# The last output store of a fused recurrence and expert block: from ScalarE's queue to GpSimd's

## The chip, the cores and the metric

The kernel runs on one core of a Trainium2 chip. The metric is the device time of one execution in microseconds. A core has five engines with a queue of instructions each: TensorE (PE in the profile; PEld is its weight load), VectorE (DVE), ScalarE (ACT), GpSimd (POOL) and SyncE (SP). Transfers are issued by SP, ACT or POOL.

## The reference

Two blocks follow each other. The first is a gated linear recurrence with complex gates, for 4 batches, 8 heads, 768 steps and a head size of 48. The second is a dense block with a squared ReLU, on 3072 rows of 384 columns:

```
for t in range(S):
    S_re, S_im = ar*S_re - ai*S_im + kv[t], ar*S_im + ai*S_re   # state: 48 x 48 per head
    y[t] = q[t] @ S_re
x = y.transpose(0, 2, 1, 3).reshape(3072, 384)
h = x @ w_in                  # 384 -> 2048
out = max(h, 0)**2 @ w_out    # 2048 -> 384
```

## The kernel before

The 3072 rows are handled as six units of 512 rows (`NU` = 6, numbered 0 to 5). For each unit the kernel computes the recurrence in chunks, turns the result, and then runs the dense block in two groups of 256 rows (`dense(n, grp)`). From unit 1 on, the second product uses a scheme with seven block products in place of eight for most groups (`seven`, the matmuls of L1600). Its partial sums are copied out of the matmul banks by ACT (L1619) and added up by DVE (L1624) into two output tiles `ots`, one for each block of 128 rows. Each tile has two halves of `DH` = 192 columns.

Every instruction, a store too, is a step of a planner (`Plan`). A step has an engine, an estimated duration, what it reads and writes, and a rank. `Plan.order` simulates the engines: again and again it takes the engine that can start a step soonest, and on it the step with the lowest rank among those that are ready; `Plan.emit` issues the steps in that order. Ties between engines are decided by the order in which the engines are looped over. `plan.shift` adds corrections to the ranks, written out by hand.

`rows(n, grp, i, o, half)` stores an output tile. For all but the last group a whole tile of 192 KB goes out on POOL's queue (L1561). For the last group (`final`: the last unit, `grp` 1) each half of 96 KB is stored as soon as it is ready (L1556). `seven` ends with two pieces of work in this order:

```
        add(n, o0, 1, 1, b2)
        rows(n, grp, 0, o0, 1)
        rows(n, grp, 0, o0)
        add(n, o1, 0, 0, b1)
        rows(n, grp, 1, o1, 0)
```

The very last step of the arithmetic is thus the add into the first half of tile 1, and the store of `(i, half)` = (1, 0) follows it. The other three halves go out on SP's queue.

The fast path is followed by a test: a value `flag`, computed at about 674 us, says whether the inputs were in the range for which it holds. Each engine loads the flag into a register (L737), and at `with tc.If(bad > 0)` (L1771) it branches over the general path, a complete second version of the kernel that isn't run on these inputs. After the branch each engine waits for the work of its own, SP also for all transfers on the hardware queues, and POOL for those on its software queue, whose semaphores it then raises by a fixed amount (`INC_SWDGE_SEM`). At the end of the context (L1798) SP waits for everything once more, the other engines report to POOL, and POOL clears the semaphores.

Of the kernel before, what the change touches and what calls it, by code (L numbers as in the profile page):

```python
# [480 lines left out]
class Plan:  # L481
# [49 lines left out]
    def order(self):  # L531
        steps = self.steps
        users = [[] for _ in steps]
        left = []
        for n, s in enumerate(steps):
            left.append(len(s[2]))
            for d in s[2]:
                users[d].append(n)
        engines = {s[0] for s in steps}
        free = {e: 0.0 for e in engines}  # L540
        wait = {e: [] for e in engines}
        done, start, at = {}, {}, {}
        bus, warm = 0.0, 6.0
        self.fill = {}

        def ready(n):
            e = steps[n][0]
            t = 0.0
            for d in steps[n][2]:
                same = steps[d][0] == e and steps[d][5] is None  # L550
                hop = 0.0 if same else self.HOP[steps[d][0]]
                if e == "PE" and not same and done[d] > 100.0:
                    paired = steps[d][5] is not None and steps[n][6]
                    hop += self.SLACK if paired else self.MARGIN
                t = max(t, done[d] + hop)
            at[n] = t
            wait[e].append(n)

        for n in range(len(steps)):
            if not left[n]:  # L560
                ready(n)
        for _ in steps:
            best = None
            for e in engines:
                if not wait[e]:
                    continue
                t = max(free[e], min(at[n] for n in wait[e]))
                if best is None or t < best[0]:
                    best = (t, e)
            t, e = best  # L570
            n = min((n for n in wait[e] if at[n] <= t), key=lambda n: (steps[n][4], n))
            wait[e].remove(n)
            _, dur, _, _, _, wire, _ = steps[n]
            start[n] = t
            if e == "PE":

                stop = t - free[e]
                spare = [b for b in self.lives if self.spare(b, done, free[e])]
                if spare and stop > self.FILL:
                    self.fill[n] = int((stop - 0.3) / self.EACH), spare[0]  # L580
                elif stop > self.STOP:
                    warm = t + self.COLD
                if t < warm:
                    dur += min(dur, 0.5 * (warm - t))
            free[e] = t + dur
            if wire is None:
                done[n] = t + dur
            else:
                lat, size = wire
                bus = max(bus, t + dur) + size / self.RATE  # L590
                done[n] = max(bus, t + dur) + lat
            for m in users[n]:
                left[m] -= 1
                if not left[m]:
                    ready(m)
        self.start, self.done = start, done
        return sorted(start, key=lambda n: (start[n], n))
# [24 lines left out]
def fast_path(ctx, tc, q, k, v, a_re, a_im, moe_w_in, moe_w_out, out, flag):  # L622
# [27 lines left out]
    dve, pool, act, sp = nc.vector, nc.gpsimd, nc.scalar, nc.sync  # L650
# [6 lines left out]
    def sb(name, n, dtype=F32, rows=C):  # L657
        return const.tile([rows, n], dtype, name=name)
# [100 lines left out]
    def dma(q, reads, writes, fn, rank, size, lat=1.8, group=None):  # L759
        name, dur = ("POOL", 0.55) if q is pool else ("SP" if q is sp else "ACT", 0.6)  # L760
        step(name, dur, reads, writes, fn, rank, (lat, size), group)
# [722 lines left out]
    def dense(n, grp):  # L1484
# [45 lines left out]
        for i in range(2):  # L1530
            b = "d%d" % take("d", 3)
            ps = bank[b][:, 0:DM]
            for part in range(NF // 2):
                s, gt = tiles[part]

                def go(part=part, gt=gt, ps=ps, i=i):
                    for f in (2 * part, 2 * part + 1):
                        pe.matmul(ps, lhsT=gt[:, f % 2, ts(i, C)], rhs=w2[:, f],  # L1538
                                  start=(f == 0), stop=(f == NF - 1))
                step("PE", 1.3, [("g", s, i), ("g", s, 2 + i), ("w2", part)], [(b,)], go,  # L1540
                     rank)
            o = take("ot", NO)
            step("ACT", ac(DM), [(b,)], [("ot", o, 0), ("ot", o, 1)], lambda ps=ps, o=o: act.copy(
                out=ots[o], in_=ps), (0, n))
            rows(n, grp, i, o)

    def rows(n, grp, i, o, half=None):

        r = n * L + (2 * grp + i) * C
        final = n == NU - 1 and grp == 1  # L1550
        if final and half is None:
            return
        queue = (act if (i, half) == (1, 0) else sp) if final else pool
        if final:
            sl = ts(half, DH)
            dma(queue, [("ot", o, half)], [], lambda: queue.dma_start(  # L1556
                out=out[r:r + C, sl], in_=ots[o][:, sl]), (DENSE, n), C * DH * 4)
            return
        if half is not None:
            return  # L1560
        dma(queue, [("ot", o, 0), ("ot", o, 1)], [], lambda: queue.dma_start(  # L1561
            out=out[r:r + C, :], in_=ots[o]), (DENSE, n), C * DM * 4)
# [65 lines left out]
    def eight(n, grp):  # L1628

        for i in range(2):  # L1630
            b0, b1, b2 = ["d%d" % take("d", 3) for _ in range(3)]
            o = take("ot", NO)
            for h in range(2):
                half(n, b0, i, h, w_lo(0), parts_of(h, 0))
            for h in range(2):
                half(n, b1, 2 + i, h, w_up(0), parts_of(h, 1))
            copy(n, o, 1, b0)
            add(n, o, 0, 1, b1)
            for h in range(2):
                half(n, b2, i, h, w_lo(1), parts_of(h, 0), last=False)  # L1640
            for h in range(2):
                half(n, b2, 2 + i, h, w_up(1), parts_of(h, 1), first=False)
            add(n, o, 1, 1, b2)
            rows(n, grp, i, o)
# [158 lines left out]
```

## Time and profile before

| | us |
|---|---|
| median of 3 runs | 702.49 |
| lowest and highest | 701.89 and 705.13 |
| the profiled execution, own time | 705.98 |
| its span, first to last instruction | 704.2 |
| granted TensorE clock, mean | 0.994 |

All times in the profile are of the one profiled execution and count from the start of its span. The profile's page gives busy times by engine, the chain of work that ended last, the costliest groups of instructions, and the transfers with their time from issue to landing. A name with a "q" behind it (ACTq, SPq) is the engine's sequencer: branches, semaphore waits and the issues of transfers stand there and don't count as busy.

### The profile page before, as it was taken

To read this page: it belongs to the slowest core of one execution; us is meant where nothing else is said; L and a number is where in the kernel's file an instruction comes from. 1 tells how busy PE (TensorE), PEld (TensorE's weight loads), DVE (VectorE), ACT (ScalarE), POOL (GpSimd) and SP (SyncE) were. 2 spreads that over 40 slices of the span, in tenths; PEclk is the share of its full clock that TensorE was granted. 3 is DMA by queue.
4 is the path that set the end of the run, shared out by engine and by line. 5 is a ranking of instruction groups with operands and counts; after the bars stand their busy time and mean duration, and the time that the engine had idled before them with its cause. 6 is when DMAs were issued, how large, how long until landed. Compare 5 with 4: busy or idle time off the path is not lost.

```text
span 704.2 us, 12518 instructions
## 1 busy us (share of the span) xinstructions
PE 685.2 (97%) x4562; PEld 622.7 (88%) x4562; DVE 572.1 (81%) x1173; ACT 347.9 (49%) x578; POOL 175.7 (25%) x334
## 2 busy tenths in 40 slices
PE   9998889999999999999999999999999999999996
PEld 9998878767788999998998998998989989999996
DVE  5989899999888789997898598998599998337721
ACT  6693468955485534376424557324657242132230
POOL 6502553052400003305044050033130033032200
PEclk9999899999999999999999999999999999999999
DMA  9741459220630004735037570036550035288600
GB/s 276 220 178 26 105 133 292 76 68 20 171 104 23 1 13 123 197 78 155 0 96 197 127 154 12 1 91 179 136 158 1 19 86 136 65 282 282 208 2 27
DMA packets 56647, 79.58 MB, mean 113 GB/s; under 512 B 10976, under 2 KB 38752, under 8 KB 56576
## 3 DMA queue, kind: packets, MB, share of 16 engines
q0 software_dynamic: 15232, 40.72, 19.1%
q1 hardware_dynamic: 37072, 32.89, 18.4%
q10 hardware_dynamic: 4272, 5.08, 2.7%
q8 instruction: 38, 0.62, 0.4%
q14 instruction: 33, 0.27, 0.1%
HBM read 48.76 MB, written 4.72 MB: 76 GB/s over the span
## 4 chain that ended last, share of the span: by engine, by line
PE 63%; DVE 24%; DMA 4%; issue 3%; ACT 3%; SPq 1%; POOL 1%; ACTq 0%; DVEq 0%
PE d L1492 24%; PE d L1600 20%; PE sc L1400 4%; DVE f L1266 3%; PE d L1538 3%; DVE f L1280 3%; PE yp L1452 3%; PE tr L1428 2%; PE yp L1456 2%; DVE aq L1270 2%; PE tr L1492 1%; DMA aq<-in_a_im_dram 1%; DMA KC<-f 1%; PE sc L1492 1%; DVE f L992 1%
## 5 line engine op out<-in xcount | busy, mean ns | idle before, releaser
L1492 PE MATMUL d<-xT,w 128*128 128x256 f32 x1056 | 236.3, 381 | 3.1 <-issue 2.1
L1492 PEld LDWEIGHTS d<-xT,w 128*128 128x128 f32 x1056 | 199.0, 190 | 31.7 <-issue 3.5
L1600 PE MATMUL d<-w,g 128*128 128x192 f32 x768 | 132.7, 328 | 0.0
L1600 PEld LDWEIGHTS d<-w,g 128*128 128x128 f32 x768 | 124.9, 190 | 1.5 <-issue 0.9
L1523 ACT ACTIVATE g<-d 128x512 f32<-128x512 f32 x88 | 52.1, 592 | 120.6 <-PE d L1492 88.9
L1321 POOL DMA_DIRECT2D KC<-f x160 | 78.4, 498 | 112.0 <-issue 56.0
L1561 POOL DMA_DIRECT2D out_dram<-ot x22 | 12.6, 572 | 241.4 <-DVE ot L1624 145.1
L1600 PE MATMUL d<-T,g 128*128 128x192 f32 x384 | 66.8, 327 | 0.7 <-DVE g L1615 0.7
L1600 PEld LDWEIGHTS d<-T,g 128*128 128x128 f32 x384 | 62.8, 190 | 1.3 <-DVE g L1615 1.0
L735 PE MATMUL d<-ident 128*128 128x128 f32 x520 | 61.1, 281 | 1.5 <-POOL ident masks.py:199 1.5
L910 POOL DMA_DIRECT2D v<-in_v_dram x80 | 46.4, 587 | 64.7 <-PE yp L1452 21.0
L1524 ACT ACTIVATE g<-g 128x512 f32<-128x512 f32 x96 | 60.5, 631 | 3.0
L735 PEld LDWEIGHTS d<-ident 128*128 128x128 f32 x520 | 60.5, 198 | 1.5 <-POOL ident masks.py:199 1.5
L1615 DVE TENSOR_TENSOR g<-g 128x512 f32<-128x512 f32 x64 | 43.1, 684 | 22.3 <-ACT g L1524 15.3
L1400 PE MATMUL sc<-QT 96*128 96x128 f32 x368 | 47.9, 285 | 1.2 <-ACT QT L1386 1.2
L1462 ACT COPY yt<-yp 112x512 f32<-112x512 f32 x24 | 26.1, 1089 | 43.5 <-PE yp L1456 43.5
L1400 PEld LDWEIGHTS sc<-QT 96*128 96x128 f32 x368 | 45.0, 198 | 3.0 <-ACT QT L1386 1.6
L1266 DVE TENSOR_TENSOR f<-aq,xn 128x384 f32<-128x384 f32 (+1 forms) x64 | 45.0, 748 | 2.0 <-ACT xn L1227 1.9
L1280 DVE TENSOR_TENSOR f<-aq 128x384 f32<-128x384 f32 (+1 forms) x64 | 44.9, 752 | 0.6
L1538 PE MATMUL d<-w,g 128*128 128x384 f32 x128 | 44.3, 488 | 0.0
L1403 DVE TENSOR_TENSOR A<-sc,mask 128x512 f32<-128x512 f32 x45 | 29.7, 680 | 15.1 <-PE sc L1400 15.0
L992 DVE TENSOR_TENSOR f<-aq 128x384 f32<-128x384 f32 x72 | 36.9, 553 | 0.9
(195 smaller groups left out, 993.5 us busy)
## 6 DMA issues: line engine op xcount, KB each, us to landing
QT<-aq SPq DMA_DIRECT2D x128, 64.0 KB, 2.1
f<-in_moe_w_in_dram POOLq DMA_DIRECT2D x8, 768.0 KB, 7.1
f<-in_moe_w_out_dram POOLq DMA_DIRECT2D x8, 768.0 KB, 6.4
KC<-f POOLq DMA_DIRECT2D x104, 48.0 KB, 2.7
out_dram<-ot POOLq DMA_DIRECT2D x22, 192.0 KB, 2.4
QT<-aq ACTq DMA_DIRECT2D x64, 64.0 KB, 2.5
v<-in_v_dram POOLq DMA_DIRECT2D x80, 48.0 KB, 2.9
xT<-yt SPq DMA_DIRECT2D x36, 96.0 KB, 2.4
```

The lines of the kernel that those rows point to most:

```text
L735: plan = Plan(lambda b: pe.matmul(bank[b][:, 0:C], lhsT=ident, rhs=ident, start=True, stop=True), ["d2", "d1", "d0"], lambda ap: tc.nc.val ...
L910: lambda i=i, c=c, src=src: pool.dma_start(out=t[32 * c:32 * c + 32, i], in_=src[c]), vrank, 32 * 1536, 4.0,
L992: dve.tensor_tensor(out=f, in0=a[:, :, :, c - 1], in1=a[:, j, :, c].unsqueeze(1).to_broadcast([C, 2, HH, D]), op=ALU.mult)
L1266: lambda j=j, r=r: dve.tensor_tensor(out=f4[:, j, r], in0=a[:, r], in1=over(j), op=ALU.mult), late[z])
L1280: lambda j=j, r=r, o=o: dve.tensor_tensor(out=o[:, :, :, r * D:(r + 1) * D], in0=qk[:, j], in1=a[:, r], op=ALU.mult), late[z])
L1321: lambda i=i, c=c, queue=queue: queue.dma_start(out=kc[32 * c:32 * c + 32, i], in_=nat[32 * i:32 * i + 32, c]),
L1400: pe.matmul(sa[:, j], lhsT=T[:, j, 1, h], rhs=T[:, j, 0, h], start=True, stop=True)
L1492: pe.matmul(ps, lhsT=w1[:, f // FP, m, ts(f % FP, C)], rhs=xT[:, n % 2, m, ts(grp, G)], start=(m == 0), stop=(m == NM - 1))
L1523: act.activation(out=o, in_=ps, func=AF.Relu)
L1524: act.activation(out=o, in_=o, func=AF.Square)
L1538: pe.matmul(ps, lhsT=gt[:, f % 2, ts(i, C)], rhs=w2[:, f], start=(f == 0), stop=(f == NF - 1))
L1600: pe.matmul(bank[b][:, 0:DH], lhsT=g4[:, r, j], rhs=w(j), start=first and j == 0, stop=last and j == NT - 1)
```

## The change

The store of `(i, half)` = (1, 0) in the last group is issued on POOL's queue in place of ACT's. It still waits for the add before it. The planner's engines become a fixed tuple in place of a set made from the steps, so that ties are decided in a fixed order.

```diff
@@ Plan.order
-        engines = {s[0] for s in steps}
+        engines = ("PE", "DVE", "POOL", "SP", "ACT")
@@ rows
         final = n == NU - 1 and grp == 1
         if final and half is None:
             return
-        queue = (act if (i, half) == (1, 0) else sp) if final else pool
+        queue = (pool if (i, half) == (1, 0) else sp) if final else pool
```

In the queues of the engines this takes one store from ACT, where it stood between the flag load and the branch, and puts it on POOL between the flag load and the branch.

## The prediction

> **What bounds the kernel now.** The change touches one transfer at the end of the program, so I read the shares first, then the chain that ended last, then the last microseconds engine by engine. From the page:
>
> ```profile
> span 704.2 us, 12518 instructions
> ...
> PE 685.2 (97%) x4562; PEld 622.7 (88%) x4562; DVE 572.1 (81%) x1173; ACT 347.9 (49%) x578; POOL 175.7 (25%) x334
> ...
> PE 63%; DVE 24%; DMA 4%; issue 3%; ACT 3%; SPq 1%; POOL 1%; ACTq 0%; DVEq 0%
> ...
> out_dram<-ot POOLq DMA_DIRECT2D x22, 192.0 KB, 2.4
> ...
> out_dram<-ot SPq DMA_DIRECT2D x3, 96.0 KB, 1.7
> out_dram<-ot ACTq DMA_DIRECT2D x1, 96.0 KB, 2.3
> ```
>
> TensorE is 97% busy: nothing that happens beside its work is worth much. The three store rows are the prices of the same kind of transfer on three queues; the single ACTq row is the one that moves. The timeline from 690 us on (start, duration, engine, line, operation) shows where it stands:
>
> ```profile
> 695.12 2.76 PE L1600 MATMUL d<-T,g 128*128 128x192 f32 x16
> ...
> 697.92 0.35 DVE L1624 TENSOR_TENSOR ot<-ot,d 128x192 f32<-128x192 f32 x1 [2.24 <-PE d L1600]
> 698.31 0.38 ACTq L1556 DMA_DIRECT2D out_dram<-ot  x1
> ```
>
> The last matmuls end at 697.9, the last add at 697.92 + 0.35 = 698.27, the store is issued 0.04 us later and lands 2.3 us after that, at 700.6. The span ends at 704.2. So 5.9 us follow the last arithmetic, and the store explains less than half of them. The rest is the closing of the program: every engine jumps over the fallback code (L1771, the `tc.If`), then all meet (L1798, the end of the context). The instructions of these two lines (count, durations in ns, first and last start):
>
> ```profile
> L1771 SPq EVENT_SEMAPHORE  x8: 17/17/17, 699.6 to 700.7; - x8
> L1771 POOLq EVENT_SEMAPHORE  x5: 17/43/43, 678.0 to 678.3; - x5
> L1771 POOLq COMPARE_BRANCH  x1: 54/54/54, 675.1 to 675.1; - x1
> L1771 POOLq INC_SWDGE_SEM  x1: 516/516/516, 678.4 to 678.4; - x1
> ...
> L1771 SPq COMPARE_BRANCH  x1: 50/50/50, 697.0 to 697.0; - x1
> ...
> L1771 ACTq COMPARE_BRANCH  x1: 58/58/58, 698.7 to 698.7; - x1
> ...
> L1771 ACTq EVENT_SEMAPHORE  x1: 17/17/17, 702.5 to 702.5; - x1
> ```
>
> ```profile
> L1798 POOLq EVENT_SEMAPHORE  x4: 17/17/17, 703.4 to 704.1; - x4
> L1798 POOLq DRAIN  x3: 46/103/1365, 678.9 to 703.9; - x3
> ```
>
> And SP's own part of L1798 in the stretch from 702.5 to 703.4 us:
>
> ```profile
> L1798 SPq EVENT_SEMAPHORE  x10: 28/28/28, 702.6 to 703.2; - x10
> ```
>
> A branch is short, but the engine's next instruction comes late: 2.6 us on SP (697.0 to 699.6), 2.9 on POOL (675.1 to 678.0), 3.8 on ACT (698.7 to 702.5). SP then waits for every transfer in turn, stands still once more between 700.8 and 702.6, and closes at 703.3; POOL, which gathers the others, goes on at 703.4 and the span ends 0.8 us later. **SP ends the kernel now**; ACT, done by 702.6, has 0.7 us to spare. POOL had finished its branch and its own closing work 24 us earlier, beside the matmuls. That cover is what the change takes away.
>
> **What the Trainium skill says.** "Runtime: NRT & Kernel Launch", section "Instruction fetch mechanics": a taken branch whose target isn't in the engine's loaded window stalls it until the target has been fetched. The trace agrees: 2.6 to 3.8 us after each of these branches. "DMA: Bandwidth & Descriptors", section "Latency and other measured facts", puts the first byte at about 0.6 us for a hardware queue and about 1 us for GpSimd's; the trace shows the issue at 0.38 us on ACT and 0.57 on POOL, and landings of 2.3 and 2.4. "Trainium Kernel Development and Optimization", section "Key Constraints": all three queues share the same 16 DMA engines, so another queue saves issue time alone. No row here contradicts it.
>
> **The change, part by part.**
>
> *The planner's fixed list of engines in place of a set* decides ties in the order in which steps are emitted. Engine by engine the two programs have the same instructions in the same order, except for this one store. Cost nothing; no work has to hide it.
>
> *Removed from ACT*: one issue of 0.38 us at 698.3, and the wait before the branch. ACT's branch moves to just after its flag load at 683.6, so its 3.8 us are covered by matmuls. What it gains is 0.7 us behind SP's path: nothing now.
>
> *Added to POOL*: the same 128 descriptors of 768 bytes. POOL loads the flag at 674.5 as before, and then, in place of the branch, waits 24 us for the last add. Only the branch and the closing instructions stand behind it on POOL; all earlier POOL transfers are out by 660. The durations are those of POOL's own rows:
>
> - The last add ends at 698.27. From an add to POOL's store: 0.3 us (add from 658.7 for 0.354, store at 659.34, for the output row block before). Start 698.6.
> - One software issue: 0.57 us (median 568 ns over twenty stores of twice the size; the number of descriptors is the same). End 699.1.
> - Branch 0.1 us later (as after the flag load, 675.0 to 675.1): 699.2. Next instruction 2.9 us on: 702.1.
> - Waits and the closing of the software semaphores: 678.0 to 678.9, 0.9 us: 703.0.
> - The 1.37 us drain: 704.4. POOL can gather then, where it did at 703.4. **Sum: +1.0 us**, and 0.8 us to the end as before: span 705.2.
>
> The store itself lands at 698.6 + 2.4 = 701.0, before POOL asks for it at 702.4: hidden by the branch, and if that cover were gone the landing would count from there. SP waits for the software semaphores that POOL raises at the end of the 0.9 us, at 703.0, and has 0.1 + 0.7 us of waits after them: 703.8, behind POOL's drain. After the change POOL is late, then SP, then nobody.
>
> *Unknowns.* The trace has no branch of POOL taken while a store flies. POOL's own 2.9 us was taken in quiet. The shortest, SP's 2.6, gives +0.7; the longest, ACT's 3.8, taken beside its own store, gives +1.9. I keep 2.9 for the point. The drain: POOL's other two took 46 and 103 ns. Was 1.37 us work, or the fetch of what came next? If it shrinks to 0.1, SP ends the kernel at 703.8 and the change costs +0.4 to +0.5. If SP's second standstill (1.8 us from 700.8 to 702.6) comes only once it is past its first waits, it starts at 703.1: 703.0 + 0.1 + 1.8 + 0.7 = 705.6, +2.2. A gain is bounded by reason: after 698.27 there are the issue, a branch and the gathering on any queue; with ACT's fetch out of SP's way the most I can name is some of that 1.8 us, and POOL would have to close by 703.3 for it to count. With the slow branch as well it is +3.1. So the bounds are -0.5 and +3.1, with +1.0 taken.
>
> **Against which time.** The profiled execution took 705.98 us: the span of 704.2 and 1.8 around it. The median of the runs shown is 702.49 (701.89 to 705.13), 3.5 below the profiled one. The change adds to either; I put it on the median: 702.49 + 1.0 = **703.5**.
>
> **The rivals.**
>
> *SP still ends the kernel, POOL's closing fits almost beside it.* For it: POOL's short drains. Against it: the 1.37 us one stands exactly there, and POOL reaches it only at 703.0. Time: +0 to +0.5, 702.5 to 703.0. Chance 0.18.
>
> *The software store lands late (slower).* Place: POOL's wait for its own store, after the branch. Landings of POOL's stores reach 4.7 us, and 6.9 for the last two before this one, at 657 and 659, which shared the engines with 768 KB loads. POOL asks 3.8 us after the issue began; from there every microsecond counts in full, and 6.3 us is the point from which the total passes 3.5 us. At 6.9 us: 1.0 + 3.1 = +4.1, 706.6. Against it: no other large transfer runs after 697, and quiet landings are 2.1 to 2.4. The slow branch with SP's second standstill comes to +3.1, just short of that point; a little lateness on top passes it. Chance 0.17.
>
> *A gain.* ACT's branch and its fetch leave the end, and SP's standstill shortens. At best -0.5, 702.0; more would have to come from around the span, which nothing shows. Chance 0.07.
>
> That the change doesn't do what it says: the store does stand on POOL's queue, behind the flag load and ahead of the branch, so I give this nothing.
>
> **How the numbers follow.** The forecast, an end later by 0.5 to 3.1 us because of POOL, has 0.58. Half a per cent is 3.5 us, about what a measurement of this kernel can tell from no change. Forecast, first rival and a small gain all lie within it: same 0.78. Slower is the late-landing rival, 0.17; faster 0.05, the part of the last rival that I can't bound by the trace. The range: -0.5 on the low side with some of the spread of the runs (0.6 below their median) gives 701.7; the high side takes +3.1 and 0.7 of the upper spread (2.6), or most of the late landing, 706.3.
>
> **What would show it.** Right: POOL's store at 698.6 for about 0.57 us, POOL's branch at 699.2 and its next instruction near 702.1, its long drain ending after SP's last wait, the closing about 1 us later, ACT's branch near 684; all before 698 unchanged. Wrong: POOL closing before SP does (first rival), the store landing more than 3.8 us after its issue (second), or a drain that is short. A difference over 3.5 us with the last add still at 698.3 and the end within 8 us of it would lie outside the span, and my argument would not cover it.

## The result and the profile after

The changed kernel takes 705.67 us (median of 20 runs, 702.98 to 707.63), the kernel before 703.54 in 20 runs (701.89 to 705.67). The ratio is **1.0028, 95% interval 1.0018 to 1.0038**: slower by 2.0 us (1.3 to 2.7). That is within half a per cent, and a ratio of 1 lies outside the interval.

The profiled execution took 706.46 us with a span of 704.6; before it was 704.2. The two spans, 0.4 us apart, hide most of the difference. First the timeline of the changed kernel near its end (start, duration, engine, line, operation, idle time before it):

```profile
694.13 2.76 PE L1600 MATMUL d<-T,g 128*128 128x192 f32 x16
...
696.93 0.35 DVE L1624 TENSOR_TENSOR ot<-ot,d 128x192 f32<-128x192 f32 x1 [2.25 <-PE d L1600]
697.58 0.56 POOL L1556 DMA_DIRECT2D out_dram<-ot  x1 [38.66 <-DVE ot L1624]
```

The last add ends at 697.28; before, it ended at 698.27. Nothing ahead of it was changed, and in the ten profiles of this study, whose arithmetic is the same (one has a tiny copy more), it ends between 695.6 and 698.3: the time to that point differs by up to 2.7 us between the profiled executions. So I compare the **tail**, from the end of the last add to the end of the span: 698.27 to 704.2 is 5.9 us before, 697.28 to 704.6 is 7.3 us after, 1.4 more. And the transfer on the page:

```profile
out_dram<-ot SPq DMA_DIRECT2D x3, 96.0 KB, 1.7
out_dram<-ot POOLq DMA_DIRECT2D x1, 96.0 KB, 4.0
```

The store that moved lands 4.0 us after its issue, where ScalarE's took 2.3. The closing, L1771 (the branch over the general path) and L1798 (the end of the context), count, durations in ns, first and last start:

```profile
L1771 SPq EVENT_SEMAPHORE  x8: 17/17/17, 698.8 to 699.3; - x8
L1771 POOLq EVENT_SEMAPHORE  x5: 17/42/43, 700.6 to 701.7; - x5
L1771 ACTq COMPARE_BRANCH  x1: 54/54/54, 683.2 to 683.2; - x1
...
L1771 POOLq COMPARE_BRANCH  x1: 50/50/50, 697.6 to 697.6; - x1
...
L1771 POOLq INC_SWDGE_SEM  x1: 536/536/536, 701.8 to 701.8; - x1
```

```profile
L1798 SPq EVENT_SEMAPHORE  x14: 17/28/28, 702.3 to 704.6; - x14
L1798 POOLq EVENT_SEMAPHORE  x4: 17/17/17, 703.9 to 704.5; - x4
L1798 POOLq DRAIN  x3: 46/103/1451, 702.4 to 704.4; - x3
L1798 SPq DRAIN  x3: 7/7/13, 703.4 to 704.1; - x3
```

ACT is past its branch by 686. POOL branches at 697.6, has its next instruction at 700.6, waits until 701.7 for its transfers, closes the software semaphores by 702.4, drains for 1.45 us, and gathers the others at 703.9. SP stood from 699.3 until POOL had raised the software semaphores (701.8 + 0.54 = 702.3) and was through its own waits at 703.4. POOL ends the kernel now: it gathers 6.6 us after the last add, where it was 5.1 before.

### The profile page after: what moved, and what is told of

Same layout as the page of the kernel before. It is cut to its first block, busy times and chain, and to the rows that moved or that the text cites. A ratio compares the mean times of both kernels' runs of the same rounds, so it can differ in the third digit from the quotient of the medians.

```text
span 704.6 us, 12517 instructions
## 1 busy us (share of the span) xinstructions
PE 685.3 (97%) x4562; PEld 621.6 (88%) x4562; DVE 571.9 (81%) x1173; ACT 347.9 (49%) x578; POOL 176.3 (25%) x335
## 4 chain that ended last, share of the span: by engine, by line
PE 67%; DVE 23%; issue 5%; DMA 2%; ACT 2%; SPq 1%; DVEq 0%; POOLq 0%; POOL 0%; ACTq 0%
PE d L1492 26%; PE d L1600 21%; PE sc L1400 5%; PE d L1538 3%; PE yp L1452 3%; PE tr L1428 3%; DVE f L1280 3%; DVE f L1266 3%; PE yp L1456 2%; PE tr L1492 2%; DVE aq L1270 1%; DMA aq<-in_a_im_dram 1%; PE sc L1492 1%; DVE f L992 1%; DVE aq L977 1%
```

## The experiments

Each was timed beside the kernel before. The edits are to the line that picks the queue unless another is shown.

**The planner's tuple alone.**

```diff
-        engines = {s[0] for s in steps}
+        engines = ("PE", "DVE", "POOL", "SP", "ACT")
```

> The planner's fixed tuple alone, with the last store on ScalarE as before. The tail is counted from the end of the last add to the end of the span: 5.9 us before, 7.3 us after the change. My theory (GpSimd's branch and closing, now behind the last add, end the kernel): tail 5.9 us, ratio 1.000. Rival (the tuple shifts the order of some step and that costs): ratio about 1.003, with the difference ahead of the last add.

Measured: ratio 1.000 (0.9989 to 1.0010). The tuple costs nothing that shows (at most 0.7 us by the interval), so the store is what the change is about. This run also gave a second profile of the order of instructions before, and there the tail was 702.5 - 697.33 = 5.2 us and not 5.9. SP's part of L1798 in its stretch from 698 to 700 us, and then in that from 699.9 to 702 us:

```profile
L1798 SPq EVENT_SEMAPHORE  x2: 28/28/28, 699.6 to 699.7; - x2
```

```profile
L1798 SPq EVENT_SEMAPHORE  x11: 17/28/28, 701.0 to 701.9; - x11
```

SP's second standstill lasted from 699.7 to 701.0, 1.3 us; in the profile before it was 1.8 (700.8 to 702.6). It ended 2.4 us after SP's first instruction behind the branch (698.6), and 3.0 us after it (699.6) in the profile before. POOL could gather 4.4 us after the last add here, at 701.7.

**POOL late, without a store of its own.** The last store stays on ACT, and POOL gets a copy of one column that waits for the last add:

```diff
     verdict()
+    o = (take("ot", NO) + 1) % NO
+    step("POOL", 0.1, [("ot", o, 0)], [("late",)], lambda: pool.tensor_copy(
+        out=few[:, 0:1], in_=ots[o][:, 0:1]), (LATE, 100))
```

> Before, with the last store left on ScalarE; GpSimd gets one tiny copy (128 x 1) that waits for the last add, ahead of its branch. No software transfer is added, only lateness of GpSimd. My theory (the late branch, the 0.5 us closing of the software semaphores and the 1.4 us drain end the kernel): copy 0.3 us after the add, next instruction 3.0 us after the branch, waits and closing 0.9, drain 1.4, gathering 5.6 to 5.7 us after the add where it was 5.1: tail 6.5 us, ratio 1.001. Rival (the late landing of the software store alone costs): tail 5.9 us, ratio 1.000.

Measured: 1.0019 (1.0008 to 1.0029), 1.3 us slower; tail 702.8 - 696.01 = 6.8 us. The closing of this kernel (its lines are four further down, L1775 and L1802):

```profile
L1775 POOLq EVENT_SEMAPHORE  x5: 17/43/43, 699.6 to 699.9; - x5
...
L1775 POOLq COMPARE_BRANCH  x1: 54/54/54, 696.1 to 696.1; - x1
```

```profile
L1802 POOLq EVENT_SEMAPHORE  x4: 17/17/17, 702.0 to 702.7; - x4
L1802 POOLq DRAIN  x3: 46/103/1365, 700.6 to 702.5; - x3
```

From branch to next instruction 3.5 us here, in place of the 3.0 that I expected; then the same waits, the same drain, gathering 6.0 us after the add. By the point values, a late POOL with no software store of the last group in flight costs about two thirds of what the change costs (the intervals overlap); what makes up the rest is not taken apart by a run. The rival, that only the landing costs, falls.

**A software store one step earlier.** The last store on ACT, the one before it on POOL:

```diff
-        queue = (act if (i, half) == (1, 0) else sp) if final else pool
+        queue = (act if (i, half) == (1, 0) else pool if (i, half) == (0, 1) else sp) if final else pool
```

> Before, with the store of (i, half) = (0, 1), the last but one, on GpSimd in place of SyncE; the last stays on ScalarE. My theory: GpSimd's 6.6 us from add to gathering start 2.6 us earlier and are over 4.0 us after the last add, ahead of SyncE; SyncE's branch moves up by 2 us as well, so that ScalarE (4.3 us after the last add) ends the kernel: tail 5.2 to 5.9 us, ratio 0.999 to 1.000. Rival (any software store in the last group costs, by its landing or its semaphores): tail 7 us or more, ratio 1.002.

Measured: 0.9989 (0.9977 to 1.0002), not told apart from no change; tail 700.9 - 696.01 = 4.9 us, less than I expected. POOL has the same store, the same 1.45 us drain and the same closing, only 2.6 us earlier:

```profile
L1798 POOLq DRAIN  x3: 46/103/1451, 698.1 to 700.6; - x3
...
L1798 ACTq DRAIN  x2: 8/8/8, 700.0 to 700.3; - x2
```

Its drain ends at 698.1 + 1.45 = 699.6; ACT reports at 700.0 and is the one waited for. A store on GpSimd's queue is not dear in itself: one step earlier it costs nothing that shows, and as the last 2.0 us.

**SyncE's last store taken away from it.** Both late stores on ACT:

```diff
+        queue = (act if half is not None and (i, half) in ((0, 1), (1, 0)) else sp) if final else pool
```

> Before, with the store of (i, half) = (0, 1) on ScalarE too, so that SyncE's last store is (1, 1) and its branch comes some 2 us earlier. My theory (who branches last ends the kernel): ScalarE ends it 4.3 us after the last add where SyncE did at 5.1: tail 5.2 us, ratio 0.999. Rival (SyncE's standstill of 1.8 us starts only when it is past the landing of the last store, and stays where it was): tail 5.9 us, ratio 1.000.

Measured: **0.9985 (0.9976 to 0.9995), 1.1 us faster than before**, by the point values the fastest version with the test in place; tail 699.9 - 695.61 = 4.3 us, lower than the 5.2 I expected, because ACT's next instruction came 2.9 us after its branch (696.0 to 698.9) and not 3.8. SP's branch stands at 692.1:

```profile
L1771 SPq EVENT_SEMAPHORE  x8: 17/17/17, 694.6 to 697.8; - x8
...
L1771 ACTq COMPARE_BRANCH  x1: 58/58/58, 696.0 to 696.0; - x1
...
L1771 ACTq EVENT_SEMAPHORE  x1: 17/17/17, 698.9 to 698.9; - x1
```

SP waits for landings until 697.8, has no stop of over 0.4 us after that, and is through at 699.0, level with ACT. Taking late work from SP made the kernel faster, though ACT got it: this shows from the other side that SP ended the kernel before.

**All four stores on SyncE.**

```diff
+        queue = sp if final else pool
```

> Before, with the last store on SyncE too, so that all four halves of the last group go out there and SyncE loads the flag and branches after the last of them. My theory (the engine that branches last pays its whole closing behind the last add): branch 1.3 us after the add, next instruction 2.6 later, eight waits, SyncE's second standstill ending 2.4 to 3.1 us after that first instruction, 0.7 us of waits: tail 7.8 to 8.5 us where the program before has 5.2 to 5.9, ratio 1.003 to 1.004. Rival (only a software store is dear, a hardware queue is a hardware queue): tail as before, ratio 1.000.

Measured: 1.0037 (1.0022 to 1.0051), 2.6 us slower (1.5 to 3.6), in the range expected. This is the least certain of the figures: it rests on 10 runs, the medians lie only 1.8 us apart, and the tail of the profile, 705.1 - 698.24 = 6.9 us, was about a microsecond under the range. SP loads the flag while it waits for the last add, so that its branch stands 0.4 us behind the add and not 1.3. SP's closing, first L1771 and then L1798 in the stretch from 702.1 to 704.2 us:

```profile
L1771 SPq EVENT_SEMAPHORE  x8: 17/17/17, 701.3 to 701.9; - x8
L1771 SPq COMPARE_BRANCH  x1: 50/50/50, 698.7 to 698.7; - x1
```

```profile
L1798 SPq EVENT_SEMAPHORE  x11: 28/28/28, 703.5 to 704.1; - x11
```

SP's second standstill is here too, from 702.0 to 703.5, 2.2 us after its first instruction, although ACT had been past its branch since 686.8: it is not a wait for ACT. A hardware queue as the last one can be as dear as GpSimd's: from its branch SP needs 5.5 us to the end of its waits, and in the two profiles of the order before 5.6 and 6.3, about as long as POOL's closing after its branch (5.9 POOL late, 6.3 in the changed kernel).

**Without the test and the branch**, first with ACT's store, then with POOL's. The general path, the flag loads and the branch are left out:

```diff
-    with tc.If(bad > 0):
-        general_path(tc, *args)
```

> Before without the test and its branch: the general path, the flag loads and the jump are left out, the fast path with the last store on ScalarE is all there. My theory (the branch's fetch is most of the tail): the store lands 2.2 us after the add, SyncE's last waits and the gathering follow: tail 3.0 to 3.4 us, ratio 0.996 to 0.997.

> The changed kernel without the test and its branch, as in the run beside it: the general path, the flag loads and the jump are left out. With no branch on GpSimd there is no fetch, no closing of the software semaphores at the branch's end, and its drain begins right after the issue, beside the landing. My theory: the store starts 0.3 us after the add, lands at 2.5, SyncE has 0.6 us of waits behind it: tail 3.8 to 4.2 us, 0.4 to 0.9 us over the run with ScalarE's store, ratio between the two about 1.001. Rival (a software store lands late by itself, 4.0 us after its issue as in the profile after the change): tail 5.5 us, over 2 us more than with ScalarE's store, ratio between the two 1.003.

Measured: 0.9964 (0.9953 to 0.9974) and 0.9980 (0.9970 to 0.9989) of the kernel before, medians 701.46 and 702.78 us: 1.3 us apart. Tails 698.4 - 695.80 = 2.6 and 699.9 - 696.06 = 3.8 us. The difference, 1.2 in the tails and 1.3 in the medians, is larger than my 0.4 to 0.9 and smaller than the rival's 2; the intervals of the two ratios are too wide to tell it from either, so the landings have to decide. The second tail is as expected; the miss is in the first, where I had let ACT's store land 2.2 us after the add, as it does with the branch. The times from issue to landing of the last group's stores, smallest, median and largest, of the kernels with ACT's and with POOL's store last:

```profile
DMA to landing us min/median/max: 1.6/1.7/1.7
```

```profile
DMA to landing us min/median/max: 1.6/1.7/1.9
```

No store is late there. ACT's needs 1.7 us where it took 2.3 before, POOL's 1.9 where it took 4.0. The rival, that a software store lands late by itself, falls. In the profile with POOL's store, SP is through 0.6 us after that landing, where with ACT's it was through 0.1 us after: SP's wait for POOL's store stands early in its list, with nine more behind it, and that for ACT's stands last. The drains of POOL and SP, again of ACT's run and then of POOL's (L1796 is the end of the context here):

```profile
L1796 POOLq DRAIN  x3: 46/103/1371, 672.1 to 698.2; - x3
L1796 SPq DRAIN  x3: 7/7/13, 697.6 to 697.9; - x3
```

```profile
L1796 POOLq DRAIN  x3: 46/108/2695, 696.3 to 699.6; - x3
L1796 SPq DRAIN  x3: 7/7/13, 698.9 to 699.3; - x3
```

With ACT's store last the long drain stands at 672, beside the matmuls, and takes 1371 ns, although no branch over the general path is there: 6 ns from the 1365 of the kernel before. The times from a branch to the next instruction differ by up to a microsecond in these traces, so I read the drain as POOL's own work and not as a fetch; what that work is, no run shows. With POOL's store last it starts with the store and lasts 2.7 us, to 699.0, just behind SP's 698.9. Issue and a drain of 1.45 us would make 2.0 of that; the other 0.7 is not explained.

Without the branch the move from ACT to POOL thus still costs 1.3 us by the medians, where it costs 2.0 with it; the spread of the runs doesn't tell these apart. Most of the cost, by these values, doesn't need the branch: with the test in place every version pays one near the end on some engine, and what sets POOL apart is the later store and the rest of its closing.

**The changed kernel with SyncE early.** The last store on POOL, the one before it on ACT:

```diff
+        queue = (pool if (i, half) == (1, 0) else act if (i, half) == (0, 1) else sp) if final else pool
```

> The changed kernel (last store on GpSimd), with the store of (i, half) = (0, 1) moved from SyncE to ScalarE. With ScalarE's store last, that move took 1.0 us off. My theory (after the change GpSimd alone ends the kernel): SyncE's earlier branch gains nothing, tail 6.5 to 7.4 us, ratio to before 1.002 to 1.003, as the change itself. Rival (SyncE ends the kernel after the change too): tail shorter by about 1 us, ratio 1.001.

Measured: 1.0023 (1.0012 to 1.0035), tail 704.1 - 697.15 = 7.0 us. The move that took 1.1 us off with ACT's store last shows no clear gain here (the two intervals overlap). The rival's ratio of 1.001 lies just outside the interval; the order in the profile says it more plainly. SP is through its waits at 702.9 and POOL gathers at 703.3, so SP isn't what the changed kernel waits for. POOL's closing:

```profile
L1771 POOLq EVENT_SEMAPHORE  x5: 17/43/43, 700.8 to 701.2; - x5
...
L1771 POOLq COMPARE_BRANCH  x1: 50/50/50, 697.4 to 697.4; - x1
```

Here POOL's five waits take 0.4 us; in the profile of the changed kernel they took 1.1. The landing cost 0.7 us there and nothing here: it comes and goes.

## Why the prediction was right

The direction, the mechanism and the size class held: slower by less than half a per cent, POOL the last to close. The point was +1.0 us, and the measured +2.0 (1.3 to 2.7) lies inside its range (0.5 to 3.1), above the point. In absolute time the miss is larger, 705.67 against 703.5 us: half of it is the base, since the 3 runs before gave 702.49 and 20 gave 703.54, and half the size of the change. The half per cent that I took for the least that can be told from no change was too coarse: the interval reaches 0.7 us to either side. By its steps, each counted from the end of the last add, with the changed kernel's profile beside it:

- *Store at +0.3*: held, 697.58 - 697.28 = 0.3.
- *Issue 0.57, branch behind it at +0.9*: the issue held (0.56), the order did not. POOL's sequencer takes the branch at 697.6, while the issue still runs on POOL (697.58 to 698.14). This step was 0.65 us too dear.
- *2.9 us to the next instruction*: 3.0 here, 3.4 with SyncE early. Held for the changed kernel, a little short for the other.
- *0.9 us of waits and closing*: 1.8 (700.6 to 702.4). The landing was to be hidden by the branch. It was not: the branch came earlier, and the last part of the store landed 4.0 us after its issue. The five waits stretched to 1.1 us. In the run with SyncE early it was hidden.
- *The 1.37 us drain, and whether it is work*: 1.45, and it did not shrink. That it is work is the reading which fits best, not shown. It is 1365 or 1371 ns where no software store stands just ahead, in quiet or at the end, with the branch or without it, and 1451 with such a store ahead of the branch.
- *Gathering 6.1 us after the add*: 6.6 in the changed kernel, 6.2 with SyncE early. The two wrong steps, 0.65 us too much and 0.9 too little, nearly cancel; that this sum came out close is in part luck.

The term that was mis-sized is the other side of the difference. I took 5.1 us, POOL's gathering in the one profile before, as what the kernel before needs. The second profile of the same order of instructions has 4.4, because SP's second standstill was over 2.4 us after its first instruction behind the branch in place of 3.0. Against 4.4 the same 6.2 to 6.6 give +1.8 to +2.2, and that is what was measured. Two profiles can't say which of the two is the common case, but the other runs point to the second. The tail of a run less its measured difference from the kernel before is an estimate of the tail before. It is 5.3 us from the changed kernel (7.3 - 2.0), and lies between 5.1 and 5.7 for seven of the eight versions that differ from it in the end; only all stores on SyncE gives less, 4.3. By this estimate the 5.9 of the profile before was long, and the 5.2 of the second one, with gathering at 4.4, nearer to the usual. It is an argument from profiles of single executions, not a measurement.

The rivals. *SP still ends the kernel*: wrong by the order of closing in the profile, and by the run with SyncE early. *The store lands late*: the place was right, and 4.0 us is just past the 3.8 from which I said that it would count, but POOL stood waiting from 700.7 on, 3.2 us after the issue, because its branch came early, and the price stayed under a microsecond. *A gain*: none; ACT's earlier branch let nothing end sooner. The unknown on SP's second standstill is answered in part: in the run with both late stores on ACT, SP waits at L1771 until 2.2 us after the add and still has no stop of over 0.4 us behind it. So the standstill isn't tied to the landing: where it was seen it ended 2.2 to 3.0 us after SP's first instruction behind the branch, and where SP's waits lasted longer than that it was hidden. What SP fetches or does in it, no run shows.

The statement of the Trainium skill ("Runtime: NRT & Kernel Launch", section "Instruction fetch mechanics") that a taken branch out of the loaded window stalls the engine until its target is fetched carried the prediction. The runs without the branch put a number on it for this kernel: 2.5 us of 704 (1 - 0.9964) with the same last store, the flag loads and the waits at the end of the branch included.

## What to carry to other kernels

After the last arithmetic a program still has a closing, and each engine's part of it starts when that engine's own last instruction is out. So give the last store to the engine whose closing is shortest, and take late work away from all others. Here the closing, from the branch on, took 2.9 to 3.9 us on ScalarE, 5.5 to 6.3 on SyncE and 5.9 to 6.3 on GpSimd where these branched near the end; against the kernel before, GpSimd last was 2.0 us slower, SyncE last 2.6 us slower (1.5 to 3.6), and ScalarE with both late stores 1.1 us faster. When an effect of this size is costed, compare tails from one fixed event and use more than one profile of the kernel before: one pair of spans showed 0.4 us of a difference of 2.

## What was not expected

- The last part of a store can land far behind the rest while engines branch. In the changed kernel 14 of the 16 reports of the store that moved came within 0.15 us, 1.8 to 1.9 us after the issue, the other two at 2.6 and 4.0. With SyncE early the last came at 3.4, without the branch at 1.9. The other queues show it too: ACT's last store took 2.3 us before, 3.1 with POOL late and 1.7 without the branch, and SyncE's last 3.2 before, 3.3 after and 1.6 without the branch. From 694 us on, the trace of the changed kernel has nine packets that fetch instructions, and those of the two versions without the branch have none. That fetch and store meet on one DMA engine would explain it; that is argued, not shown.
- A software store is taken up 0.3 us after the add that it waits for; the tiny copy on the same engine started 0.07 us after it (696.08 against 696.01).
- The time from a branch to an engine's next instruction isn't a constant of the engine: on POOL 2.5 us (674.2 to 676.7, tuple alone) and 2.9 (before) with the branch far from the end, 2.8 with the store one step earlier, 3.0 to 3.5 with it at the end; on ACT 2.5 (after, 683.2 to 685.7) to 3.8 (before).
